# One written list of steps for the work ahead of ab, and four-square scores for pairs 2 to 4

## The chip, the cores and the metric

The kernel runs on one core of a Trainium2 chip, in one launch. The metric is the device time of that launch in microseconds (us); lower is better. The kernel before takes 846.54 us (median of 3 runs, 845.32 to 847.07).

## The reference

Inputs are q, k, v of 4 batches, 8 heads, 576 positions and 64 channels, and six float32 weight matrices, which the host lays out as 64-bit words. Cut to what is computed:

```python
scores = q @ k.T / sqrt(64) - slope[h] * abs(i - j)     # only 0 <= i - j < 128 counts
attn = softmax(scores) @ v                              # 4 x 8 x 576 x 64
x = attn as (2304, 512)
h = (x @ w1) * (x @ w2) @ w3                            # 2304 x 1024
x = h @ w_out                                           # 2304 x 512
h = x @ w_in                                            # 2304 x 2048
out = (h * clip(h + 3, 0, 6) / 6) @ w_out2              # 2304 x 512
```

## The kernel before

Heads are taken two at a time, so there are 16 pairs `n`, four to a batch; 64 channels of one head and 64 of the other fill the 128 partitions. Tokens go through the dense layers in five chunks of 512 (the last of 256), and a chunk needs the four pairs of its batch.

For a pair, `products` (L148 to L163) computes scores in 64-row squares: query square i against the up to three key squares that its window reaches, nine squares i for two heads, in two parts (squares 0 to 5 and 6 to 8), one PSUM tile each (`s`). Each is a 64 by 64 use of the TensorE array, placed by `tile_position`. For pairs 0 to 4 head h sits on rows and columns h of the array, so two corners of the array are used. From pair 5 on, a second copy of q and k with the two heads exchanged (`other`, tiles `qo` and `ko`, filled by two half transfers each) serves the odd squares i, so all four corners are in use. `scores` (L167) adds the position bias and finds the minimum on VectorE (tile `mn`), then ScalarE exponentiates (`pr`). `normalize` (L180) takes a reciprocal on VectorE (`rc`) and multiplies on GpSimd. `pt` (L198) transposes the probabilities by 64 by 64 matmuls against an identity and copies them out of PSUM (`th`, one half by ScalarE, one by VectorE). `pv` (L224) multiplies by v (`X`), copies the sum out (`xf`), and `x_parts` splits it into a high and a low float32r part (`x`). The `s`, `pt` and `X` tiles of all pairs share three PSUM tiles of two banks, by `bank2`.

Dense products are done as three float32r matmuls (`mm3`, L52 to L55: high by high, high by low, low by high). Weights come as 64-bit words: `unpack` (L57 to L74) makes float32 from them with one ScalarE instruction (L66) and two on VectorE (L67, L71); `split` (L76) then makes the two parts, one copy on ScalarE (L77) and one subtraction on VectorE (L78).

Ahead of the first dense chunk w3 and w_out are multiplied into one matrix W: eight row blocks (`w_half`, L383 to L398, tile `wps`, two PSUM banks in turn shared with `ab`), each in two halves; blocks 0 and 1 by plain float32 (L393), 2 to 7 by `mm3`. Then for chunk k the loop `block` gives pieces of `ab_unit` (two products of x by w1 and w2, tile `ab`; the first is copied to `asb` by ScalarE, the second multiplied with it on VectorE and split into `g`) and `y_unit` (g by W, tile `y`), with the next batch's pairs put between the pieces by `gaps`. After three such chunks and two without attention the last layers follow (`h` and `o`).

What sets the order: within `block` TensorE's instructions keep the order in which the code is written. Ahead of `ab`, in the part that this change is about, the order of every engine is left to a scheduler, which ranks the instructions of `attn_slot` and of the list `work` by its own cost model; `work` and `FILL` only say in which order the code hands them over. DMAs are issued by SyncE (SP), one after another; an issue that waits holds those behind it. A raw weight tile (`raw`) is one of three buffers.

Of the kernel before, what the change touches and what calls it, by code (L numbers as in the profile page):

```python
# [23 lines left out]
def tile_attention_moe_moe2(ctx: ExitStack, tc: tile.TileContext, qT, kT, vm, vt, wo, w3, w12, w2x, out):  # L24
# [26 lines left out]

    def mm3(ps, lh, ll, rh, rl, first, last, pinned=False, **kw):  # L52
        in_order(pinned, nc.tensor.matmul(ps, lh, rh, start=first, stop=False, **kw))  # L53
        in_order(pinned, nc.tensor.matmul(ps, lh, rl, start=False, stop=False, **kw))  # L54
        in_order(pinned, nc.tensor.matmul(ps, ll, rh, start=False, stop=last, **kw))  # L55

    def unpack(raw, out=None, pinned=False):  # L57
# [8 lines left out]
        in_order(pinned, nc.scalar.activation(w1f, w1f, AF.Prelu, scale=2.0 ** -112, alpha=-(2.0 ** 32)))  # L66
        in_order(pinned, nc.vector.tensor_scalar(  # L67
# [63 lines left out]
    other = {}  # L131
# [47 lines left out]

    def normalize(n, js):  # L180
        _, sm, rc = stat[n]
        cols = slice(js[0], js[-1] + 1)
        nc.vector.tensor_scalar_add(rc[:, cols], sm[:, cols], 1e-9)
        nc.vector.reciprocal(rc[:, cols], rc[:, cols])
        for i in js:
            o = prob[n, i][:, SPAN - width(i) :]
            nc.gpsimd.tensor_scalar(  # L187
                out=o, in0=o, scalar1=rc[:, i : i + 1], scalar2=1.0, op0=ALU.mult, op1=ALU.mult
            )
# [8 lines left out]
    def pt(n, g):  # L198

        t = bank2(n, 2 - 2 * g, f"pt_{n}_{g}")  # L200
# [5 lines left out]
        for pair in zip_longest(*blocks):  # L206
            for ik in pair:
                for h in range(2):
# [8 lines left out]
                    ))  # L217
        ths = [a1.tile([P, 2 * SPAN], F32, tag="th", bufs=4, name=f"th_{n}_{h}_{g}") for h in range(2)]
        for h in range(2):
            (nc.vector.tensor_copy if h else nc.scalar.copy)(ths[h], t[:, h, 0 : 2 * SPAN])  # L220
        pts[n, g] = ths

    def pv(n):
# [23 lines left out]
        x = a1.tile([P, S], F32, tag="xf", bufs=NP + 1, name=f"xf_{n}")  # L247
        nc.scalar.copy(x, X[0][:, 0:S])
        nc.vector.tensor_tensor(out=x[:, D:S], in0=X[1][:, D:S], in1=x[:, D:S], op=ALU.add)
        x_parts(n, x)  # L250
# [22 lines left out]
    SLOTS = 6  # L273

    def loads(n, nm):
        if n != NP - 1 and n + 1 < NHP:
            load_hp(n + 1 if n >= NP else n + 2, nm)

    def attn_slot(g):
        n, s = divmod(g, SLOTS)  # L280
        if s == 0:
            if n > 0:
                pv(n - 1)
            products(n, 0)
            scores(n, (0, 1, 2))
        elif s == 1:
            normalize(n, (0, 1, 2))
            if 0 < n < NP:
                load_hp(n + 1, "v")
            scores(n, (3, 4, 5))  # L290
            products(n, 1)
        elif s == 2:
            normalize(n, (3, 4, 5))
            scores(n, (6, 7, 8))
            normalize(n, (6, 7, 8))
        elif s in (3, 4):
            pt(n, s - 3)
            loads(n, "qk"[s - 3])

    def pair_steps(n):  # L300

        if n == NP:
            yield from (lambda s=s: attn_slot(SLOTS * n + s) for s in (2, 3, 4))
        else:

            def first():
                for part in range(2):
                    products(n, part)
                for js in ((0, 1, 2), (3, 4, 5), (6, 7, 8)):
                    scores(n, js)  # L310
                    normalize(n, js)

            def second():
                pt(n, 0)
                loads(n, "q")
                pt(n, 1)
                loads(n, "k")

            yield first
            yield second  # L320
        yield lambda: pv(n)
# [12 lines left out]
    def load_wo(i):  # L334
        rawt["wo", i] = rawo[i // 2][:, i % 2, :]
        nc.sync.dma_start(out=rawt["wo", i], in_=wo[i])

    def load(key, src, *pools):
# [4 lines left out]
        nc.sync.dma_start(out=rawt[key], in_=src)  # L343
# [40 lines left out]
    def w_half(i, half):  # L384
# [6 lines left out]
        for m in range(half * KH, (half + 1) * KH):  # L391
            if i < WHOLE:
                nc.tensor.matmul(ps[:, 0:DM], w3v[i][:, m, :], wof[m], start=m == 0, stop=m == KF - 1)  # L393
                continue
            hi, lo = w3v[i]
            mm3(ps[:, 0:DM], hi[:, m, :], lo[:, m, :], *wov[m], m == 0, m == KF - 1)
        if half == 1:
            split(W["h"][:, i, :], W["l"][:, i, :], ps[:, 0:DM], nc.vector)  # L398

    load_hp(0, "qk")  # L400
# [13 lines left out]
    queue = [("w3", i) for i in range(KF)] + [("w12", f) for f in range(W12_EARLY)]  # L414
    nxt = 0

    def more():
        nonlocal nxt
        if nxt < len(queue):
            k, i = queue[nxt]  # L420
            load((k, i), {"w3": w3, "w12": w12}[k][i], rawp, rawp, rawx)
            nxt += 1

    more()
    load_hp(1, "qk")
    load_wo(0)
    load_hp(0, "v")
    load_wo(1)
    load_hp(1, "v")
    more()  # L430
    load_wo(2)
    load_wo(3)
    more()

    work = []
    for i in range(KF):
        work += [("w3", i), ("h", i, 0), ("h", i, 1)]
    head = work.index(("w3", 2))
    work[:head] = [
        ("w3", 0), ("wo", 0), ("wo", 1), ("h", 0, 0), ("w3", 1), ("h", 1, 0),  # L440
        ("wo", 2), ("wo", 3), ("h", 0, 1), ("h", 1, 1),
    ]
    a = work.index(("h", WHOLE - 1, 1)) + 1
    work[a:a] = [("ws", i) for i in range(KH)]
    for f in range(W12_EARLY):
        work.insert(work.index(("h", KH + 1 + f, 1)) + 1 if f < KH - 1 else len(work), ("w12", f))
# [492 lines left out]
```

## Time and profile before

| | us |
|---|---|
| median of 3 runs | 846.54 |
| the profiled execution | 845.8 |
| its span, first to last instruction | 844.0 |
| TensorE busy in the span | 824.2 (98%) |
| VectorE busy | 466.4 (55%) |
| ScalarE busy | 378.4 (45%) |
| GpSimd busy | 98.1 (12%) |
| start of the first `ab` matmul | 100.47 |

The profile counts a matmul as busy from its issue to its modelled end, and matmuls are pipelined, so that consecutive ones overlap. Busy time alone thus doesn't tell how fast TensorE works; the starts of the rows and the granted clock (1.00 is 2.4 GHz, 0.50 is 1.2 GHz) do. A float32 matmul is recorded twice or more, so a pair's 18 score matmuls are 36 records.

### The profile page before, as it was taken

The numbers are of one execution on the slowest core, as the hardware profiler recorded it, in microseconds if no ns is written. First come the engines' busy times: TensorE is split into PE (matmuls) and PEld (weight loads), VectorE is DVE, ScalarE is ACT, GpSimd is POOL, SyncE is SP. The second block draws the span as 40 slices with busy tenths as digits, with TensorE's granted clock in tenths as the row PEclk, the third lists the DMA queues.
The fourth block names the chain that finished last, engine by engine and source line by source line (L and its number), as shares of the span: only waits on it lengthen the run. The fifth ranks groups of instructions, "written<-read, shape, count | busy, mean of one in ns | idle before, by whom it ended". The sixth has DMA issues, their size and how long they took to land.

```text
span 844.0 us, 15817 instructions
## 1 busy us (share of the span) xinstructions
PE 824.2 (98%) x6304; PEld 698.5 (83%) x6304; DVE 466.4 (55%) x1054; ACT 378.4 (45%) x820; POOL 98.1 (12%) x185
## 2 busy tenths in 40 slices
PE   5989999999999999999999999999999999999998
PEld 4567777888888788888899898998889889898886
DVE  5985477425452454246573877885543547443543
ACT  7765565525441445224352654555332335332333
POOL 3333303222231222300000000000000000000000
PEclk9989999999999999999999999999999999999999
DMA  9753543334332332316666589589855377455502
GB/s 352 284 217 100 162 137 102 99 100 114 95 91 73 104 81 62 125 64 237 261 194 239 229 333 363 160 303 390 326 196 215 138 274 293 189 208 203 188 1 75
DMA packets 42841, 155.62 MB, mean 184 GB/s; under 512 B 4880, under 2 KB 20240, under 8 KB 31504
## 3 DMA queue, kind: packets, MB, share of 16 engines
q1 hardware_dynamic: 42768, 154.62, 51.2%
q8 instruction: 49, 0.80, 0.4%
q14 instruction: 24, 0.20, 0.1%
HBM read 118.55 MB, written 36.04 MB: 183 GB/s over the span
## 4 chain that ended last, share of the span: by engine, by line
PE 91%; DVE 4%; ACT 2%; DMA 1%; issue 1%; POOL 0%; SPq 0%; DVEq 0%; POOLq 0%
PE ab L53 8%; PE o L54 8%; PE o L55 8%; PE o L53 8%; PE ab L54 8%; PE ab L55 7%; PE h L53 7%; PE h L54 7%; PE h L55 7%; PE y L53 4%; PE y L54 4%; PE y L55 4%; PE s L159 3%; PE X L241 3%; PE pt L214 3%; DMA raww<-in_w_dram 1%
## 5 line engine op out<-in xcount | busy, mean ns | idle before, releaser
L53 PE MATMUL ab<-x,w12h 128*128 128x512 f32 (+1 forms) x320 | 121.3, 379 | 0.4 <-ACT asb L517 0.4
L54 PE MATMUL ab<-x,w12h 128*128 128x512 f32 (+1 forms) x320 | 118.1, 369 | 0.0
L55 PE MATMUL ab<-x,w12l 128*128 128x512 f32 (+1 forms) x320 | 117.9, 369 | 0.0
L53 PE MATMUL h<-yh,va 128*128 128x384 f32 x336 | 114.1, 340 | 0.2 <-DVE rl L748 0.2
L54 PE MATMUL h<-yl,va 128*128 128x384 f32 x336 | 113.3, 337 | 0.3 <-DVE yl L78 0.3
L55 PE MATMUL h<-yh,va 128*128 128x384 f32 x336 | 113.3, 337 | 0.0
L54 PE MATMUL o<-vo,g 128*128 128x512 f32 x288 | 113.2, 393 | 0.0
L53 PE MATMUL o<-vo,g 128*128 128x512 f32 x288 | 113.1, 393 | 0.0
L55 PE MATMUL o<-vo,g 128*128 128x512 f32 x288 | 87.2, 393 | 0.0
L187 POOL TENSOR_SCALAR pr<-pr,rc 128x192 f32<-128x192 f32 (+1 forms) x144 | 71.9, 519 | 131.5 <-ACT pr L178 79.1
L747 ACT ACTIVATE rl<-c,three 128x384 f32<-128x384 f32 x72 | 44.4, 617 | 79.5 <-DVE c L777 48.4
L53 PEld LDWEIGHTS ab<-x,w12h 128*128 128x128 f32 x320 | 60.4, 189 | 14.3 <-issue 2.0
L178 ACT ACTIVATE pr<-pr,mn 128x192 f32<-128x192 f32 (+1 forms) x144 | 61.3, 427 | 19.8 <-DVE mn L173 19.7
L55 PEld LDWEIGHTS ab<-x,w12l 128*128 128x128 f32 x320 | 60.4, 189 | 10.2
L53 PEld LDWEIGHTS h<-yh,va 128*128 128x128 f32 x336 | 63.1, 188 | 6.7 <-DVE rl L748 3.1
L54 PEld LDWEIGHTS ab<-x,w12h 128*128 128x128 f32 x320 | 60.4, 189 | 9.0
L54 PEld LDWEIGHTS h<-yl,va 128*128 128x128 f32 x336 | 63.1, 188 | 4.2 <-DVE yl L78 0.6
L55 PEld LDWEIGHTS h<-yh,va 128*128 128x128 f32 x336 | 63.1, 188 | 0.0
L55 PEld LDWEIGHTS o<-vo,g 128*128 128x128 f32 x288 | 53.9, 188 | 10.5 <-DVE g L78 0.3
L78 DVE TENSOR_TENSOR g<-rl,g 128x384 fp32r<-128x384 f32 x96 | 53.2, 555 | 16.8 <-ACT g L77 14.3
L53 PEld LDWEIGHTS o<-vo,g 128*128 128x128 f32 x288 | 54.1, 188 | 9.5 <-ACT g L77 0.2
L54 PEld LDWEIGHTS o<-vo,g 128*128 128x128 f32 x288 | 54.1, 188 | 9.3
(95 smaller groups left out, 1371.4 us busy)
## 6 DMA issues: line engine op xcount, KB each, us to landing
va<-vad SPq DMA_DIRECT2D x18, 1792.0 KB, 7.4
vo<-vod SPq DMA_DIRECT2D x18, 1024.0 KB, 9.5
raww<-in_w_dram SPq DMA_DIRECT2D x16, 1024.0 KB, 4.9
rawv<-in_w2x_dram SPq DMA_DIRECT2D x16, 1024.0 KB, 7.4
vad<-va SPq DMA_DIRECT2D x8, 1792.0 KB, 7.3
vod<-vo SPq DMA_DIRECT2D x8, 1024.0 KB, 10.9
yraw<-yT SPq DMA_DIRECT2D x21, 384.0 KB, 9.1
qw<-in_qT_dram SPq DMA_DIRECT2D x16, 288.0 KB, 3.9
```

What stands on the lines that cost most here:

```text
L53: in_order(pinned, nc.tensor.matmul(ps, lh, rh, start=first, stop=False, **kw))
L54: in_order(pinned, nc.tensor.matmul(ps, lh, rl, start=False, stop=False, **kw))
L55: in_order(pinned, nc.tensor.matmul(ps, ll, rh, start=False, stop=last, **kw))
L78: lo_eng.tensor_tensor(out=lo, in0=src, in1=f32(hi), op=ALU.subtract)
L159: in_order(written[0] or (a, h, i % 2) != (0, 0, 0), nc.tensor.matmul(o[HB[h], :], q[HB[r], i * D : (i + 1) * D], k[HB[r], (i + 1) * D - w ...
L178: nc.scalar.activation(o, o, AF.Exp, bias=mn[:, i : i + 1], scale=-1.0, accum_out=sm[:, i : i + 1])
L187: nc.gpsimd.tensor_scalar(out=o, in0=o, scalar1=rc[:, i : i + 1], scalar2=1.0, op0=ALU.mult, op1=ALU.mult)
L214: last_pe["pt", n, g] = in_order(written[0], nc.tensor.matmul(t[HB[c], h, o : o + D], prob[n, i][HB[h], (k - i + 2) * D : (k - i + 3) * D] ...
L241: last_pe["x", n, h] = in_order(written[0] or begun, nc.tensor.matmul(X[p][HB[h], a * D : b * D], vw[place(n)][HB[p], k // 2, HB[h]], pts[ ...
L747: nc.scalar.activation(rl, h, AF.Relu, bias=three[:, 0:1], scale=1.0)
```

## The change

1. `fx` pins instructions to the order in which they are written, on all engines. What `attn_slot`, `work`, `FILL` and `GATE` handed to the scheduler becomes one string of steps, `STEPS`, that is run from left to right; each engine keeps the order of the list. The letters: Lq, Lk, Lv, Lo, L, Lw load q, k, v, w_out, w3 and w12; S is `products`, M `scores`, R `normalize`, P the transposes and T their copies, X the product with v, E its copy, D its split; Uo, U, Uw unpack and Vo, V, Vw split weights; H is half a block of W and Z its split. S2.1 is part 1 of pair 2, M and R have three squares each, H4.0 is the first half of block 4.
2. `unit` functions are cut in two so that unpacking and splitting, transposes and copies, product and copy are steps of their own.
3. q and k are stored in DRAM in both head orders side by side; from pair 2 on one transfer brings both (576 KB instead of 288 KB). `qw` and `kw` have twice the size, `other` is gone.
4. `swap` holds from pair 2 on (before: from pair 5 on).
5. In `block`, pair 4 comes with its scores done, and `gaps` change for pairs 4 to 7.

The diff, cut to this:

```diff
+    fixed = [False]
+    def fx(ins):
+        return in_order(fixed[0], ins)
...
-        qw.append(pool.tile([P, S], F32, name=f"qw{i}"))
-        kw.append(pool.tile([P, S], F32, name=f"kw{i}"))
+        qw.append(pool.tile([P, 2, S], F32, name=f"qw{i}"))
+        kw.append(pool.tile([P, 2, S], F32, name=f"kw{i}"))
...
-                nc.sync.dma_start(out=r[place(n)], in_=src[n])
-                if n > NP:
-                    for h in range(2):
-                        nc.sync.dma_start(out=other[nm][HB[h], :], in_=src[n][HB[1 - h], :])
+                orders = slice(0, 2 if n > 1 else 1)
+                fx(nc.sync.dma_start(out=r[place(n)][:, orders, :], in_=src[n][:, orders, :]))
...
-                    swap = n > NP and i % 2 == 1
+                    swap = n > 1 and i % 2 == 1
                     r = 1 - h if swap else h
-                    q, k = (other["q"], other["k"]) if swap else (qw[place(n)], kw[place(n)])
+                    q, k = (t[place(n)][:, int(swap), :] for t in (qw, kw))
...
+    STEPS = """
+        Lk0 Lq0 S0.0 S0.1 M0.0 Lk1 Lq1 M0.1 R0.0 M0.2 S1.0 R0.1 R0.2 L0 U0 Lo0 Uo0 Lo1 P0.0 P0.1 T0.0
+        Uo1 T0.1 L1 Lv0 U1 H0.0 M1.0 X0 M1.1 R1.0 Lo2 Lo3 L2 R1.1 Uo2 E0 Uo3 H1.0 S1.1 M1.2 Lk2 Lq2 P1.0
+        T1.0 H0.1 S2.0 R1.2 Lv2 Lv1 L3 P1.1 H1.1 Lk3 U2 Vo1 Z0 V2 T1.1 X1 U3 Vo0 Vo2 Lq3 Z1 Vo3 L4 H2.0
+        H2.1 E1 V3 D0 M2.1 L5 M2.0 R2.1 S2.1 Lv3 M2.2 H3.0 R2.0 S3.0 H3.1 P2.0 R2.2 P2.1 U4 U5 V4 Z2 Z3
+        H4.0 V5 M3.0 H5.0 L6 L7 T2.1 H4.1 M3.1 R3.1 U6 U7 T2.0 Z4 V6 H5.1 Lq4 R3.0 X2 Z5 Lw0 V7 H6.0 E2
+        S3.1 Lv4 Uw0 Lw1 D1 Lk4 M3.2 H7.0 P3.0 H6.1 R3.2 P3.1 Vw0 D2 Lw2 T3.0 S4.0 Uw1 T3.1 X3 H7.1 Vw1
+        E3 Z6 S4.1 D3 M4.0 M4.2 M4.1 R4.2 Uw2 R4.0 Z7 R4.1 Vw2
+    """
...
+    written[0] = fixed[0] = True
+    for s in STEPS.split():
+        name = s.rstrip("0123456789.")
+        does[name](*map(int, s[len(name) :].split(".")))
+    fixed[0] = False
...
-            steps = list(pair_steps(n))
-            gaps = (3, 1, 1, 1) if n == NP else (4, 1, 1) if n == NP + 1 else (3, 1, 1)
-            for step, gap in zip(steps, gaps):
-                step()
+            late = k == 0
+            if n > NP:
+                first(n, 0)
+                first(n, 1)
+            gaps = (3, 1, 1) if n == NP else (4, 2, 1) if n == NP + 1 else (3, 1 + late, 1)
+            for step, gap in zip((None, second, pv), gaps):
+                if step:
+                    step(n)
                 for _ in range(gap):
                     yield next(work)
```

How instructions move, at the two places that the prediction rests on. First ScalarE around the start of `ab`, in the built program before (`w12h` and `raww_3` are a weight block of `ab`, `Wh` the high part of W, `pr_6` to `pr_8` the last squares of pair 4, `asb` the copy of the first `ab` product):

```order
L77 CAST w12h_1087<-raww_2_933 128x1024
L77 CAST Wh<-wps_964 128x512
L248 COPY xf_1015<-X_2_991 128x576
L77 CAST x_3_1018<-xf_1015 128x512
L77 CAST x_0_1339<-xf_345 128x64
L77 CAST Wh<-wps_1060 128x512
L178 ACTIVATE pr_6_1138,sm_1035<-pr_6_1138,mn_1034 128x192
L178 ACTIVATE pr_7_1141,sm_1035<-pr_7_1141,mn_1034 128x192
L178 ACTIVATE pr_8_1144,sm_1035<-pr_8_1144,mn_1034 128x192
L517 COPY asb_0_1165<-ab_0_0_1152 128x512
```

and the same place in the changed program, from the last six of the nine exponentials of pair 4 on:

```order
L180 ACTIVATE pr_6_1092,sm_1081<-pr_6_1092,mn_1080 128x192
L180 ACTIVATE pr_7_1095,sm_1081<-pr_7_1095,mn_1080 128x192
L180 ACTIVATE pr_8_1098,sm_1081<-pr_8_1098,mn_1080 128x192
L180 ACTIVATE pr_3_1101,sm_1081<-pr_3_1101,mn_1080 128x192
L180 ACTIVATE pr_4_1104,sm_1081<-pr_4_1104,mn_1080 128x192
L180 ACTIVATE pr_5_1107,sm_1081<-pr_5_1107,mn_1080 128x192
L71 ACTIVATE raww_2_999<-raww_2_999 128x1024
L82 CAST Wh<-wps_912 128x512
L484 COPY asb_0_1160<-ab_0_0_1147 128x512
```

The high part of the last W block and the copy `asb` now stand behind all nine exponentials of pair 4 and the unpacking of the third w12 block; before, six of the exponentials and that unpacking were ahead of both.

Second, VectorE where the first weights are unpacked, before (`raww_1` and `raww_2` are w3 blocks, `rawol` the w_out blocks 2 and 3, `wov` unpacked w_out and `wovl` its low part, `th` a copy of transposes of pair 0):

```order
L67 TENSOR_SCALAR raww_1_134<-raww_1_134 128x1024
L183 TENSOR_SCALAR rc_366<-sm_365 128x3
L184 RECIPROCAL rc_366<-rc_366 128x3
L71 SCALAR_TENSOR_TENSOR w3v_226<-raww_1_134 128x1024
L184 RECIPROCAL rc_366<-rc_366 128x3
L78 TENSOR_TENSOR wovl_377<-wov_196,wovh_376 128x1024
L220 COPY th_1_0_263<-pt_0_237 128x384
L67 TENSOR_SCALAR rawol<-rawol 128x1024
L71 SCALAR_TENSOR_TENSOR wov_267<-rawol 128x1024
```

and in the changed program from the last reciprocal of pair 0 on (`raww_0` is w3 block 0, `rawoh` the w_out blocks 0 and 1):

```order
L186 RECIPROCAL rc_146<-rc_146 128x3
L72 TENSOR_SCALAR raww_0_204<-raww_0_204 128x1024
L76 SCALAR_TENSOR_TENSOR w3v_206<-raww_0_204 128x1024
L72 TENSOR_SCALAR rawoh<-rawoh 128x1024
L76 SCALAR_TENSOR_TENSOR wov_211<-rawoh 128x1024
L227 COPY th_1_0_267<-pt_0_216 128x384
L72 TENSOR_SCALAR rawoh<-rawoh 128x1024
L76 SCALAR_TENSOR_TENSOR wov_270<-rawoh 128x1024
L227 COPY th_1_1_275<-pt_1_241 128x384
L72 TENSOR_SCALAR raww_1_278<-raww_1_278 128x1024
L76 SCALAR_TENSOR_TENSOR w3v_282<-raww_1_278 128x1024
```

The copies of pair 0's transposes now stand between the first four unpackings, and no low part is made among them; before, two low parts of w_out and the third to sixth unpacking came ahead of the second copy.

## Rows read from the trace of the kernel before

**Rows 1.** Two stretches: start, length, busy us (records) by engine, granted clock, DMA

```profile
0.00:100.47 100.47, 87.04 (x917) 63.45 (x917) 70.85 (x176) 65.30 (x146) 34.30 (x56) 0.95 0.59 220
100.47:844.00 743.53, 737.20 (x5390) 635.06 (x5388) 395.52 (x879) 313.07 (x674) 63.81 (x129) 1.00 0.51 180
```

**Rows 2.** TensorE's waits over the span: us, times, longest

```profile
PE s L159 <- DMA kw<-in_kT_dram: 4.6, 1, 4.6
PE s L159 <- DVE rc L184: 2.6, 1, 2.6
PE X L241 <- DVE th L220: 2.5, 3, 1.2
PE pt L214 <- POOL pr L187: 2.3, 3, 1.5
PE wps L393 <- DVE wov L71: 2.0, 1, 2.0
```

**Rows 3.** Stretches, counting score instructions alone; first number after length is TensorE

```profile
86.00:88.00 2.00, 1.88 (x24) 1.53 (x24) 0.00 (x0) 0.00 (x0) 1.00 0.00 0
99.30:100.50 1.20, 1.16 (x12) 0.79 (x12) 0.00 (x0) 0.00 (x0) 1.00 1.01 430
145.10:146.70 1.60, 1.59 (x36) 1.28 (x36) 0.00 (x0) 0.00 (x0) 1.00 0.00 1
```

**Rows 4.** Timeline of TensorE: start, length, work, records

```profile
22.97 3.70 PE L393 MATMUL wps<-wov,w3v 128*128 128x512 f32 x8
...
81.20 1.54 PE L241 MATMUL X<-th,vw 64*64 64x192 f32 x40
...
108.86 0.93 PE L214 MATMUL pt<-ident,pr 64*64 64x64 f32 x48
```

**Rows 5.** Stretches around TensorE's idle times, columns as in rows 1

```profile
12.59:17.00 4.41, 4.41 (x46) 3.68 (x47) 3.37 (x10) 3.54 (x9) 4.25 (x7) 0.61 1.01 385
...
18.79:20.79 2.00, 0.00 (x0) 0.00 (x1) 2.00 (x8) 2.00 (x9) 0.00 (x0) 1.00 1.03 418
20.79:23.00 2.21, 2.21 (x11) 0.91 (x11) 2.21 (x7) 1.55 (x2) 1.27 (x2) 1.00 1.01 419
50.03:54.44 4.41, 1.35 (x29) 0.73 (x29) 3.96 (x8) 3.44 (x6) 2.75 (x3) 1.00 0.48 197
54.44:61.30 6.86, 6.86 (x32) 5.26 (x33) 5.27 (x18) 4.32 (x12) 1.47 (x2) 0.50 0.45 153
```

**Rows 6.** The same view from the first `ab` matmul on

```profile
100.47:108.80 8.33, 8.33 (x38) 6.68 (x36) 3.26 (x12) 3.71 (x9) 1.23 (x3) 1.00 0.64 173
```

**Rows 7.** Groups on VectorE and ScalarE ahead of 100.47: busy us, mean ns, idle before

```profile
L173 DVE CUSTOM_DVE_ANT_0 pr<-s,rel 128x192 f32<-128x192 f32 (+2 forms) x42 | 11.5, 327 | 2.3 <-PE s L159 2.1 <-POOL pr L187 0.2
L71 DVE SCALAR_TENSOR_TENSOR raww<-raww 128x1024 int32<-128x1024 int32 x9 | 11.0, 1220 | 0.8 <-ACT raww L66 0.6
L67 DVE TENSOR_SCALAR raww<-raww 128x1024 int32<-128x1024 int32 x11 | 8.7, 794 | 10.2 <-DMA raww<-in_w_dram 10.2
L78 DVE TENSOR_TENSOR w3l<-raww,w3h 128x1024 fp32r<-128x1024 f32 x6 | 7.4, 1234 | 0.6 <-ACT w3h L77 0.6
...
L178 ACT ACTIVATE pr<-pr,mn 128x192 f32<-128x192 f32 (+2 forms) x42 | 17.9, 430 | 6.9 <-DVE mn L173 6.9
L66 ACT ACTIVATE raww<-raww 128x1024 f32<-128x1024 f32 x11 | 13.0, 1178 | 7.6 <-DMA raww<-in_w_dram 7.6
...
L77 ACT CAST Wh<-wps 128x512 fp32r<-128x512 f32 x8 | 4.6, 574 | 2.9 <-PE wps L55 2.9
```

**Rows 8.** Timeline of GpSimd, columns as in rows 4

```profile
12.75 5.22 POOL L187 TENSOR_SCALAR pr<-pr,rc 128x64 f32<-128x64 f32 x9 [10.44 <-DVE rc L184]
21.73 7.52 POOL L187 TENSOR_SCALAR pr<-pr,rc 128x64 f32<-128x64 f32 x6 [3.76 <-DVE rc L184]
```

**Rows 9.** TensorE's waits from 100 us on

```profile
PE X L241 <- DVE th L220: 1.3, 2, 1.1
```

**Rows 10.** Stretch from 32 to 100 us, columns as in rows 1

```profile
32.00:100.00 68.00, 63.74 (x718) 49.24 (x719) 47.87 (x117) 40.64 (x93) 19.88 (x31) 0.95 0.43 149
```

More of the change, by code (lines that the diff above doesn't have):

```diff
@@ L196, in parity, with squares @@
         return 1 if k == NQ - 1 else k % 2
-    def pt(n, g):
-        t = bank2(n, 2 - 2 * g, f"pt_{n}_{g}")
+    ptb = {}
+    def squares(n, g):
+        ptb[n, g] = t = bank2(n, 2 - 2 * g, f"pt_{n}_{g}")
         blocks = ([], [])
@@ L246, in pv, with joined @@
                     begun.add(key)
[L247 to L250, printed above, removed]
+        Xb[n] = X
+    def joined(n):
+        X = Xb.pop(n)
+        xf[n] = x = a1.tile([P, S], F32, tag="xf", bufs=NP + 1, name=f"xf_{n}")
+        fx(nc.scalar.copy(x, X[0][:, 0:S]))
+        fx(nc.vector.tensor_tensor(out=x[:, D:S], in0=X[1][:, D:S], in1=x[:, D:S], op=ALU.add))
+    def pv(n):
+        weighted(n)
+        joined(n)
+        x_parts(n, xf.pop(n))
         if NP <= n < NHP - 1:
@@ L271, in x_parts, with first, second @@
             xs[B, c] = (t[:, c % 2, 0, :], t[:, c % 2, 1, :])
-    SLOTS = 6
     def loads(n, nm):
         if n != NP - 1 and n + 1 < NHP:
[L277 to L321, printed above, removed]
+            load_hp(n + 1, nm)
+    def first(n, part):
+        products(n, part)
+        for js in ((6, 7, 8),) if part else ((0, 1, 2), (3, 4, 5)):
+            scores(n, js)
+            normalize(n, js)
+    def second(n):
+        pt(n, 0)
+        loads(n, "q")
+        pt(n, 1)
+        loads(n, "k")
     flat = lambda t: t.rearrange("p a b -> p (a b)")
@@ L413, in tile_attention_moe_moe2 @@
     nc.gpsimd.memset(three, 3.0)
[L414 to L446, printed above, removed]
@@ L466, in tile_attention_moe_moe2 @@
-    wi = 0
-    end = work.index(("h", KF - 2, 0))
-    for s in range(nslot):
-        attn_slot(s)
-        upto = FILL[s] if s in FILL else FILL[4] + (s + 1 - len(FILL)) * (end - FILL[4]) // (SLOTS * NP - 2 - len(FILL))
-        if s >= SLOTS * NP - 2:
-            upto = work.index(("h", KF - 2, 1)) + 1
-        if s >= SLOTS * NP:
-            upto = len(work)
-        while wi < min(upto, len(work)):
-            do_work(work[wi])
-            wi += 1
+    STEPS = """
[6 more added lines that the diff above has]
+        E3 Z6 S4.1 D3 M4.0 M4.2 M4.1 R4.2 Uw2 R4.0 Z7 R4.1 Vw2
@@ new lines, in tile_attention_moe_moe2 @@
+    """
+    PARTS3 = ((0, 1, 2), (3, 4, 5), (6, 7, 8))
+    does = {
+        "Lq": lambda n: load_hp(n, "q"),
+        "Lk": lambda n: load_hp(n, "k"),
+        "Lv": lambda n: load_hp(n, "v"),
+        "Lo": load_wo,
+        "L": lambda i: load(("w3", i), w3[i], rawp, rawp, rawx),
+        "Lw": lambda f: load(("w12", f), w12[f], rawp, rawp, rawx),
+        "S": products,
+        "M": lambda n, u: scores(n, PARTS3[u]),
+        "R": lambda n, u: normalize(n, PARTS3[u]),
+        "P": squares,
+        "T": copies,
+        "X": weighted,
+        "E": joined,
+        "D": lambda n: x_parts(n, xf.pop(n)),
+        "Uo": wo_unit,
+        "Vo": wo_split,
+        "U": w3_unpack,
+        "V": w3_split,
+        "Uw": w12_unpack,
+        "Vw": w12_split,
+        "H": w_half,
+        "Z": w_row,
+    }
```

95 lines of the change are left out of this document (45 added, 50 removed).

## The prediction

> **What bounds the kernel now.** I read the span in two stretches first. From 100.47 us, where `ab` begins, TensorE is busy all but some 6 us of 744 at granted clock 1.00 [rows 1], and its waits over the whole span that are worth naming lie ahead of that point but for one [rows 2, 9]. So the work after 100.47 is a block of fixed length, and the question is when `ab` begins and what its first pieces wait for. Ahead of it I summed what TensorE has to do at full clock. A pair's scores by two corners take 1.88 for part 0 and 1.16 for part 1, 3.0 together [rows 3]; five pairs make 15.2. Transposes are 0.93 a half, eight halves 7.4; X is 1.54 a pair, four make 6.2; blocks 0 and 1 of W are four halves of 3.70, 14.8 [rows 4]. Blocks 2 to 7 are 144 matmuls; 36 matmuls of that size took 8.33 us, 0.231 each [rows 6], so 33.3. The sum is 76.9, and the first scores can't start before 4.6, when q and k have landed [rows 2]: `ab` could begin at 81.5 and begins at 100.5. The missing 19 us are some 9 of waits (2.6, 2.0, 2.3, 1.2 of X ahead of `ab`, small ones) and the rest slow clock: from 54.44 to 61.30 the clock was 0.50, which costs half of 6.86, 3.4 us, and from 12.59 to 17.00 it was 0.61, 1.7 us more [rows 5]; the first scores run slow too.
>
> **The change, part by part.**
>
> *Four corners for pairs 2 to 4.* All 36 records of a pair take 1.59 where four corners are used [rows 3], against 3.0. Three pairs save 4.4 us of TensorE; as the list later leaves TensorE the bound, I count all of it, inside the sum below.
>
> *Both head orders in one transfer.* Six loads ahead of `ab` grow by 288 KB, 1.8 MB in all. At the 430 GB/s of a full stretch [rows 3] that is 4 us of transfer. They are issued from some 27 us on, and from 32 to 100 us the DMA engines are busy 0.43 of the time [rows 10]. I take nothing; at worst each pair's scores wait for the second 288 KB twice, 1.4 us a pair, 4 in all. From pair 5 on the bytes are the same and issues fewer: nothing.
>
> *The list, to the first half of W.* Pair 0 starts as before at 4.6. VectorE now reduces its scores with no unpacking between; nine exponentials at 0.43 [rows 7], from some 8.7, end near 13. Unpacking starts at 13.2, instead of 8.3. Here the change loses: H0.0 starts at about 17.5, not 15.8, but pair 1's scores start at 11.4, not 12.6.
>
> *The stretch that VectorE bounds, 13 to 46 us.* Up to Vo3, after which block 2 of W can run through, the list gives VectorE eight unpackings of 0.79 + 1.22 [rows 7], 16.1; five low parts of 1.23, 6.2; nine reductions of 0.33, 3.0; eight copies and sums of half the size of a low part, 0.62 by that estimate, 5.0. That is 30.3. To it I add 2.5 for waits on ScalarE, where an unpacking stands behind six exponentials. Vo3 ends near 46. TensorE waits in this stretch (for E0 ahead of S1.1, for pair 1's normalizing ahead of P1.0, about 1.2 and 2.4), but all that it has to do by then fits. Behind VectorE's waits stand only its own steps; SP holds v of pair 1 and block 3 of w3 behind Lv2, which waits for X0 at 23, and they are needed at 40 and 38. Bounds for this stretch come from GpSimd: pair 0's nine multiplications took 0.58 each, while six of pair 1's took 1.25 each beside unpacking that kept VectorE fully busy [rows 8]. The list puts pairs 0 and 1 beside unpacking throughout. I take 0.58 for pair 0, which is multiplied mostly before the unpacking starts, and 1.25 for the six of pair 1 that stand beside it; all 18 at 0.58 would give Vo3 at 44, all 18 at 1.25 near 51, since the copies T wait for the transposes, these for GpSimd, and the unpacking behind T on VectorE for both.
>
> The Trainium skill has a rule that speaks against this placement: in "SBUF — State Buffer", section "SBUF: two separate sides", VectorE and GpSimd share one port pair, an exclusive lock, so that whoever comes second is blocked for the whole instruction. The 1.25 of rows 8 agrees with it; carried through for both pairs it is the slower rival below.
>
> *From there to `ab`: TensorE.* After 46.0 it has the second half of H2.1, 2.8; ten halves of 12 matmuls, 27.7; S2.1, S3 and S4 by four corners, 3.7; four transposes, 3.7; two X, 3.1. Sum 41.0. VectorE's remaining steps up to E3 are about 30 us beside it, so TensorE should bound; I add 1 us for V4 and Z2, which H4.0 waits for, and for X3. `ab` begins at 88.0, 12.5 earlier than before.
>
> *A wait that the change adds.* The second product of `ab` takes the PSUM bank that the copy `asb` empties. In ScalarE's row that copy now stands behind all nine exponentials of pair 4, an unpacking, and the high part of W's last block, and ScalarE is in order. The exponentials follow D3, at 87.7: nine at 0.44 end at 91.7; the unpacking takes 1.18, the high part 0.57 [rows 7], the copy about the same: 94.1. The first product (12 matmuls, 2.8) ends at 90.8. TensorE stands for 3.3 us; what is queued behind it is all of `ab`. Bounds are 2.7 (three exponentials done ahead of S4.1) and 4.6 (ScalarE late by another step). The second product starts at 94.1; before, it started at 100.5 + 2.7 = 103.2 without a wait. 9.1 are left.
>
> *The clock.* Rows 5 show both answers to an idle TensorE: 2.0 us of idle (18.79 to 20.79) left the clock at 1.00, while 3.1 us idle out of 4.41 (50.03 to 54.44) was followed by 6.86 us at 0.50. The changed program has two places of the second kind, around P1.0 (3.6 idle out of 4.6) and the wait above (3.3). I count one drop, 3.4 us: 9.1 - 3.4 = 5.7.
>
> In "TensorE: Matmul & The Clock Gate", section "Part 1: The HAM clock gate", the skill says that half rate is the default and that activity releases it. By that rule both places would drop, and the time would be the one of the two-drop rival below.
>
> *`gaps`.* X of pair 5 waited 1.3 us for its copies [rows 9], with one piece between transposes and X; now there are two, so 1.0 comes back. Pair 4's X comes two pieces earlier, its copies then have one piece, 2.8 us, against two copies and an unpacking: 0 to 0.5 lost. I count 1.0 in all: 5.7 + 1.0 = 6.7.
>
> The profiled execution was 845.8, its span 844.0 and 1.8 around it; the median is 846.54. 845.8 - 6.7 is 839.1, the median less 6.7 is 839.8. I forecast **839.5 us**.
>
> **Rivals.**
> 1. *No drop of the clock.* The waits are short of what lowered it at 50 to 54 us, or fall apart: 3.4 less, 836.1; with the short bounds of the wait and of GpSimd (0.6 and 2) 833. For it: the 2.0 us idle without a drop. Against: 3.3 is nearer to 3.1 out of 4.41.
> 2. *Two drops*: the stretch to 46 ends 2.6 later (H0.1 at half clock holds Z0 and what is behind it), and `ab` is slow too: 842 to 843.
> 3. *GpSimd held off through pairs 0 and 1*: slower. Each T on VectorE then waits for transposes that wait for 1.25 us multiplications; Vo3 comes at 51 instead of 46, `ab` at 93; with the two drops (6.0 against 3.4) the sum is 6.7 - 5 - 2.6 = -0.9, and with the long bound of the `asb` wait, -2.2: 847 to 848. It decides if block 2's second half starts later than about 52. For it: rows 8, second row. Against: pair 0 has a start of 3 us on the unpacking.
> 4. *Four squares don't run at once* in the new places: 4.4 lost, 844. Against it: pairs from 5 on are written alike and take 1.59 [rows 3].
>
> **How the numbers follow.** Forecast 0.45 (837 to 841.5), no drop 0.27, two drops 0.14, GpSimd 0.09, four squares 0.05. The range reaches down to rival 1 with its short bounds, 832.5, and up past rivals 2 and 4, 845.0; it leaves out rival 3 and the ends. 0.2%, 1.7 us, is about what a measurement of this kernel can tell from no change. Faster by more (under 844.8): the forecast, rivals 1 and 2, half of 4, less a margin, 0.85; within: 0.06; slower: rival 3, 0.09.
>
> **What would show it.** `ab` should begin between 86 and 90; S2 to S4 as 36 records in about 1.6; TensorE waits of 1 to 2.5 us for GpSimd ahead of pair 1's transposes, and of 2.7 to 4.6 for the copy `asb` at the second product of `ab`; a stretch of 6 to 7 us at 0.50 behind one of them; X of pair 5 without a wait; from pair 8 on nothing changed. I am wrong if Vo3 ends after 50, if the DMA is what TensorE waits for, or if the part from `ab` on changes in length by more than these waits and the clock.

## The result, and the profile after

The changed kernel takes 838.46 us (median of 4 runs, 837.42 to 839.42), the kernel before 845.93 beside it (4 runs, 844.83 to 847.07): a ratio of 0.991, 95% interval 0.989 to 0.993. That is 7.5 us faster. The forecast was 839.5, in a range of 832.5 to 845.0. The number was right; the experiments below show that several of its terms were not, and that they partly cancelled.

The profiled execution took 837.42 with a span of 835.5. Read as [rows 1], in two stretches around the first `ab` matmul:

```profile
0.00:88.92 88.92, 79.03 (x916) 56.67 (x917) 68.53 (x162) 60.32 (x136) 36.46 (x50) 0.96 0.67 248
88.92:835.50 746.58, 738.60 (x5390) 635.58 (x5388) 400.99 (x892) 316.91 (x685) 67.21 (x135) 1.00 0.49 181
```

`ab` begins 11.6 us earlier, and what follows is 3.1 us longer: the gain was made ahead of `ab`, and a part was handed back behind it. TensorE's waits over the span, against [rows 2] (us in total, times, longest):

```profile
PE s L161 <- DMA qw<-in_qT_dram: 4.5, 1, 4.5
PE pt L218 <- POOL pr L189: 3.2, 4, 1.5
PE ab L58 <- ACT asb L484: 2.4, 2, 2.3
PE X L255 <- DVE th L227: 1.7, 2, 1.0
```

The waits for `rc` and `wov` are gone, one of 2.3 for the copy `asb` is new, and pair 0's transposes now wait for GpSimd, 2.5 in all (before, only later pairs' did). Where the clock was low, read as [rows 5]:

```profile
12.50:15.98 3.48, 1.76 (x81) 1.49 (x81) 3.24 (x6) 3.48 (x4) 3.48 (x5) 1.00 0.99 415
15.98:22.65 6.67, 5.91 (x34) 3.02 (x35) 6.46 (x16) 2.38 (x8) 1.24 (x1) 0.50 1.03 417
22.65:26.00 3.35, 3.35 (x49) 1.89 (x49) 2.23 (x10) 3.35 (x11) 1.86 (x5) 0.98 1.00 409
91.93:94.19 2.26, 0.00 (x1) 0.00 (x0) 0.96 (x1) 2.21 (x5) 1.02 (x3) 1.00 0.68 277
94.19:97.94 3.75, 3.75 (x9) 2.93 (x10) 2.71 (x7) 1.15 (x1) 3.03 (x6) 0.54 0.00 0
```

Two stretches at 0.50: one of 6.8 us (its end lies in the third row) behind the idle time in pair 0's transposes, one of 3.4 us behind the wait for `asb`. ScalarE's row at that wait (timeline: start, length, work):

```profile
91.65 0.44 ACT L180 ACTIVATE pr<-pr,mn 128x192 f32<-128x192 f32 x1
...
92.09 1.11 ACT L71 ACTIVATE raww<-raww 128x1024 f32<-128x1024 f32 x1
93.09 0.57 ACT L82 CAST Wh<-wps 128x512 fp32r<-128x512 f32 x1
93.56 0.58 ACT L484 COPY asb<-ab 128x512 f32<-128x512 f32 x1
```

and TensorE's there and at the first half of W:

```profile
15.85 0.65 PE L218 MATMUL pt<-ident,pr 64*64 64x64 f32 x16 [1.54 <-POOL pr L189]
17.27 0.69 PE L218 MATMUL pt<-ident,pr 64*64 64x64 f32 x12 [0.76 <-POOL pr L189]
17.89 6.12 PE L388 MATMUL wps<-wov,w3v 128*128 128x512 f32 x8
...
34.51 1.10 PE L161 MATMUL s<-kw,qw 64*64 64x64 f32 x24
...
48.27 0.87 PE L161 MATMUL s<-kw,qw 64*64 64x192 f32 x12
...
94.19 0.57 PE L58 MATMUL ab<-x,w12h 128*128 128x512 f32 x1 [2.26 <-ACT asb L484]
...
107.50 1.54 PE L255 MATMUL X<-th,vw 64*64 64x192 f32 x40 [0.99 <-DVE th L227]
```

The copy stands behind the last exponential, an unpacking and `Wh`, as the order said. At half clock the first half of W takes 6.12 for what took 3.70 [rows 4].

### The profile page after: what moved, and what is told of

Read it like the earlier page. It is cut to its first block, busy times and chain, and to the rows that moved or that the text cites. A ratio compares the mean times of both kernels' runs of the same rounds, so it can differ in the third digit from the quotient of the medians.

```text
span 835.5 us, 15720 instructions
## 1 busy us (share of the span) xinstructions
PE 817.6 (98%) x6304; PEld 692.2 (83%) x6304; DVE 469.5 (56%) x1054; ACT 377.2 (45%) x820; POOL 103.7 (12%) x185
## 4 chain that ended last, share of the span: by engine, by line
PE 87%; DVE 7%; ACT 4%; issue 1%; POOL 1%; DMA 0%; SPq 0%; DVEq 0%; ACTq 0%; POOLq 0%
PE o L59 8%; PE o L60 8%; PE o L58 8%; PE ab L58 8%; PE h L58 7%; PE ab L59 7%; PE ab L60 7%; PE h L59 7%; PE h L60 7%; PE y L58 4%; PE y L59 4%; PE y L60 4%; PE s L161 3%; PE X L255 2%; ACT pr L180 2%; PE pt L218 2%
## 5 line engine op out<-in xcount | busy, mean ns | idle before, releaser
L189 POOL TENSOR_SCALAR pr<-pr,rc 128x192 f32<-128x192 f32 (+1 forms) x144 | 76.1, 549 | 116.2 <-ACT pr L180 91.2
```

The costliest lines, as they stand in the source:

```text
L189: fx(nc.gpsimd.tensor_scalar(out=o, in0=o, scalar1=rc[:, i : i + 1], scalar2=1.0, op0=ALU.mult, op1=ALU.mult))
```

## Experiments

All times below are medians; the kernel before took 845.4 to 846.4 beside them. Where ratios matter they are to the kernel before. The theory on record was that of the prediction: shorter scores, an order that lets TensorE bound from 46 us on, and two prices for it (the wait for `asb`, the clock).

### Is it the four corners?

```diff
-                    swap = n > 1 and i % 2 == 1
+                    swap = n > NP and i % 2 == 1
```

> The changed kernel with scores of pairs 2 to 4 on two corners again, all else the same, the transfers of both head orders too. Theory (TensorE bounds from 46 us on): S2, S3 and S4 take 3.0 us each instead of 1.6 to 2.0, `ab` begins 3.6 to 4.4 later, and the time is 842 to 843. Rival (VectorE or ScalarE sets the end of that stretch, four corners only make TensorE wait): 838.5 to 840. TensorE's waits for other engines ahead of `ab` don't change by the theory; by the rival they shrink by what the scores grow.

The second adds, in `load_hp`:

```diff
-                orders = slice(0, 2 if n > 1 else 1)
+                orders = slice(0, 2 if n > NP else 1)
```

> As e1_two_corners, and the loads of q and k for pairs 2 to 4 bring one head order, 288 KB instead of 576. Theory (the doubled transfers are hidden): within 0.5 us of e1_two_corners. Rival (the second 288 KB holds other loads on SP's queue): 1 to 4 us faster than e1_two_corners.

The third makes the same part of the change in the kernel before, and nothing else (`qw` and `kw` of twice the size, both orders by one transfer from pair 2 on, `swap` from pair 2 on):

> The kernel before with one part of the change alone: q and k in both head orders by one transfer, and four corners for the scores of pairs 2 to 4. Its order ahead of `ab` is still the scheduler's. Theory (after e1_two_corners: what the scores save ahead of `ab` mostly goes into waits, and the order makes the gain): 844 to 846, `ab` begins 0 to 1.5 earlier than in the kernel before. Rival (the step of the prediction: 3 times 1.4 of TensorE time come off the end): 841 to 842, `ab` begins 4 earlier.

Measured: 838.92 (837.43 to 840.72), 837.84 (837.37 to 837.97), and 847.17, which is slower than the kernel before (ratio 1.0031, interval 1.0014 to 1.0047). The changed kernel's 838.46 lies between the first two. TensorE's rows of e1_two_corners at the scores of pairs 2 and 3:

```profile
48.50 1.20 PE L161 MATMUL s<-kw,qw 64*64 64x192 f32 x12
52.58 1.90 PE L161 MATMUL s<-kw,qw 64*64 64x64 f32 x24
...
90.29 0.50 PE L58 MATMUL ab<-x,w12h 128*128 128x512 f32 x1
```

A pair's scores take 1.90 + 1.20 on two corners and 1.10 + 0.87 on four, 1.1 apart and not 1.4. From S2.1 to `ab` it is 41.8 us in e1 and 40.65 in the changed kernel (48.27 to 88.92), so of the 2.6 that the scores of that stretch grew (two parts by 0.8, three by 0.33) 1.15 arrived at `ab`; the wait of X of pair 3 (0.68) took part of the rest. The 0.8 by which S2.0 grew went into the wait for GpSimd behind it: from S2.0 to the second half of block 1 of W it is 2.97 in e1 and 2.98 in the changed kernel. With one head order (e2) the same stretch is 41.80, 47.67 to 89.47: the doubled transfers cost nothing. In the whole time the four corners can't be told from 0, by either e1 or e2: the intervals of e1 and of the changed kernel leave room for some 3.5 us at most. The runs of e1 lie in two pairs (837.4 and 837.8, 840.1 and 840.7), and the trace is of the slowest, so what it shows behind `ab` is no measure of the corners. Without the list they bring nothing: in e5 `ab` begins at 100.7. The rival of e1 holds for the time, and e5 came out even slower than its theory: this is not where the gain is.

### Is it the pinned order?

```diff
-    written[0] = fixed[0] = True
+    written[0] = fixed[0] = False
     for s in STEPS.split():
```

> The changed kernel with the same list of steps, written in the same order, but not pinned: a scheduler ranks the instructions ahead of `ab`, as in the kernel before. Theory (the pinned order of the list makes most of the gain): 842 to 846; unpacking comes back in front of pair 0's multiplications and of its copies, and TensorE's waits ahead of `ab` grow by 4 or more. Rival (the finer steps and their place in the code are enough, the pin adds nothing): 837.5 to 839.5.

Measured: 844.58 (ratio 0.9992, interval 0.9983 to 1.0001): without the pin the same steps in the same order of writing, four corners included, give nothing. The theory holds, and the pin is worth 6 to 7 us (6.1 by the medians; each was taken beside runs of its own of the kernel before, and by the ratios it is 6.8). The next two pin half of the list each; `S2.0` is the point of change:

```diff
         does[name](*map(int, s[len(name) :].split(".")))
+        if s == "S2.0":
+            written[0] = fixed[0] = False
```

> The changed kernel, pinned to the list only up to and with S2.0, the first scores of pair 2; the steps behind it are written in the same order, and a scheduler ranks them. Theory (after e6_unpinned, where S2.0 came at 44.5 instead of 34.5 and `ab` at 100.9 instead of 88.9: the gain is made ahead of S2.0, where unpacking stands behind pair 0's and pair 1's steps on VectorE): S2.0 at 34 to 36, `ab` at 89 to 92, 837 to 840. Rival (the order behind S2.0 makes it): `ab` at 98 or later, 842 to 845.

> The mirror of e9_pin_first: ranked by a scheduler up to S2.0, pinned behind it. Theory: S2.0 at 42 to 45, `ab` at 97 to 100, and then the wait for `asb` as in the changed kernel: 843 to 847. Rival: `ab` at 91 or earlier, 838 to 840.

Measured: 848.16 (ratio 1.0024, interval 1.0011 to 1.0036) and 843.45 (0.9965, 0.9954 to 0.9976). Starts in the profiled runs, and the length from `ab` to the end of the span:

| | S1.1 | S2.0 | `ab` | from `ab` on |
|---|---|---|---|---|
| before | 42.2 | 48.9 | 100.5 | 743.5 |
| unpinned | 35.8 | 44.5 | 100.9 | 741.6 |
| pinned up to S2.0 | 38.9 | 46.9 | 104.1 | 741.6 |
| pinned behind S2.0 | 31.5 | 36.0 | 95.2 | 746.5 |
| the whole list | 29.1 | 34.5 | 88.9 | 746.6 |

Only the column `ab` compares like with like, for all of W stands ahead of it in every row. Ahead of S2.0 stand three halves of blocks 0 and 1 in the last two rows and all four in the others, 3.7 us more, and in the kernel before also 41 matmuls of later blocks, 9.5 us at the 0.231 of [rows 6]. My theory of e9 fell: with its own steps pinned, S2.0 came 12.4 us later than with the whole list, 3.7 of it for that half block, and with only the later steps pinned 1.5 later. VectorE's rows tell why. The two copies of pair 0's transposes and the sum of its X in the changed kernel (timeline):

```profile
16.84 0.55 DVE L227 COPY th<-pt 128x384 f32<-128x384 f32 x1
...
19.24 0.55 DVE L227 COPY th<-pt 128x384 f32<-128x384 f32 x1
...
26.90 0.68 DVE L267 TENSOR_TENSOR xf<-X,xf 128x512 f32<-128x512 f32 x1
```

and in e9_pin_first, with what stands ahead of the copies (the last row is ScalarE's):

```profile
17.92 1.23 DVE L83 TENSOR_TENSOR wovl<-wov,wovh 128x1024 fp32r<-128x1024 f32 x1 [1.11 <-ACT wovh L82]
19.06 0.55 DVE L227 COPY th<-pt 128x384 f32<-128x384 f32 x1
...
22.65 1.23 DVE L83 TENSOR_TENSOR wovl<-wov,wovh 128x1024 fp32r<-128x1024 f32 x1 [1.11 <-ACT wovh L82]
23.79 0.55 DVE L227 COPY th<-pt 128x384 f32<-128x384 f32 x1
...
34.16 0.68 DVE L267 TENSOR_TENSOR xf<-X,xf 128x512 f32<-128x512 f32 x1
...
26.99 1.17 ACT L71 ACTIVATE raww<-raww 128x1024 f32<-128x1024 f32 x1 [2.94 <-DMA raww<-in_w_dram]
```

A pin keeps pinned instructions in order among themselves; an unpinned one may still stand between them. The low parts `wovl`, which no TensorE instruction needs before block 2 of W, come ahead of each copy of pair 0 and cost it 1.2 of work and 1.1 of waiting for ScalarE, twice. With that VectorE reaches pair 1's scores 4.6 later (26.19 for 21.63). ScalarE then takes the unpacking of the third w3 block, U2, ahead of pair 1's exponentials, when its transfer lands at 27.0, and pair 1's GpSimd work starts 6.4 us later:

```profile
30.14 4.71 POOL L189 TENSOR_SCALAR pr<-pr,rc 128x64 f32<-128x64 f32 x6 [13.04 <-DVE rc L186]
```

(23.74 in the changed kernel, below). The kernel before and e6_unpinned have low parts in the same place; there the second of these two copies starts at 33.12 and 27.32:

```profile
23.93 0.55 DVE L220 COPY th<-pt 128x384 f32<-128x384 f32 x1
33.12 0.55 DVE L220 COPY th<-pt 128x384 f32<-128x384 f32 x1
```

In e10_pin_last no low part stands there; its time lies in the range that I gave only by luck, for the reason falls with that of e9, and its `ab` is late for what happened behind S2.0: 2.7 of waits for GpSimd in pair 1's transposes instead of 0.76, and a low clock from 39.7 to 46.5, in which half a block of W took 6.20.

What the pin does, by these rows, is keep weight work that is needed late behind attention work that is needed early, on VectorE and ScalarE. No run pins one engine alone, so the share of each, and of the order of the DMA issues, stays open. The table's last column shows the price of the pinned end: some 5 us between the two kinds of order.

### The price behind `ab`

```diff
-        E3 Z6 S4.1 D3 M4.0 M4.2 M4.1 R4.2 Uw2 R4.0 Z7 R4.1 Vw2
+        E3 Z6 S4.1 D3 M4.0 Z7 M4.2 M4.1 R4.2 R4.0 R4.1 Uw2 Vw2
```

> The changed kernel with the split Z7 of W's last block moved up in the list, behind M4.0 instead of behind R4.0, and Uw2 behind R4.1. The second product of `ab` then no longer waits for the copy `asb` behind nine exponentials and an unpacking. Theory (the wait of 2.3 us and the 3.4 us of half clock behind it, worth 1.7, both come from that order): no wait at the second product, no stretch at 0.50 near 95, time 834 to 835. Rival 1 (the clock drop has another cause): 836. Rival 2 (the wait only moves on to the transposes of pair 4, whose exponentials now end 0.6 to 1.2 later, or to the third weight block, which is unpacked later): 837 to 839.

and with only Z7 moved:

```diff
+        E3 Z6 S4.1 D3 M4.0 Z7 M4.2 M4.1 R4.2 Uw2 R4.0 R4.1 Vw2
```

> As e3_z7_early, but Uw2 stays ahead of R4.0, so that the third weight block is unpacked and its buffers come free as early as in the changed kernel; only Z7 is moved. Theory (in e3_z7_early the 2.6 us wait of S5.1 came from the later transfers of the next weight blocks, whose unpacking stands on ScalarE ahead of the copy of X4): no wait of S5.1 over 0.5, 833.5 to 835. Rival (it came from the order that the scheduler then gives ScalarE after the list, whatever the transfers do): a wait of 1.5 to 3 for that copy again, 836 to 837.

Measured: 836.35 (835.61 to 836.51) and 839.12 (838.94 to 840.19). In e3 the wait at the second product is gone, and two others are there (waits, then the stretch behind the first of them):

```profile
PE s L161 <- ACT xf L266: 2.6, 1, 2.6
...
PE ab L58 <- ACT asb L484: 0.9, 1, 0.9
```

```profile
109.08:115.00 5.92, 5.92 (x27) 4.57 (x28) 5.32 (x23) 4.34 (x15) 1.52 (x2) 0.71 0.72 226
```

The medians differ by 2.1, and no run of e3 is as slow as the fastest of the changed kernel. But the two traces are only 1.2 apart (834.3 and 835.5), and 0.85 of that lies ahead of `ab`, which begins at 88.07, where the two lists are alike and the first low stretch lasted 3.4 us instead of 6.8. From `ab` on it is 746.2 for 746.6. So rival 2, that the wait moves on, took nearly all of the 4 us in the traces; the low clock now follows the 2.6. Where the rest of the 2.1 comes from they don't show. ScalarE's row shows what the copy `xf` of pair 4 stands behind:

```profile
103.59 1.16 ACT L71 ACTIVATE raww<-raww 128x1024 f32<-128x1024 f32 x1 [3.91 <-DMA raww<-in_w_dram]
104.91 0.62 ACT L82 CAST g<-asb 128x512 fp32r<-128x512 f32 x1 [0.16 <-DVE asb L490]
106.05 1.12 ACT L82 CAST w12h<-raww 128x1024 fp32r<-128x1024 f32 x1 [0.51 <-DVE raww L76]
107.32 1.21 ACT L71 ACTIVATE raww<-raww 128x1024 f32<-128x1024 f32 x1
108.42 0.61 ACT L266 COPY xf<-X 128x576 f32<-128x576 f32 x1
```

In e8 that wait is 1.0, ScalarE waits for the next weight block until 105.6, later still than the 103.6 of e3, and three other waits came (1.0 for GpSimd at pair 4's transposes, 0.7 and 1.3 for `asb`). Neither theory nor rival of e8 holds; what sets the landing of those blocks is open.

### `gaps`

```diff
-            gaps = (3, 1, 1) if n == NP else (4, 2, 1) if n == NP + 1 else (3, 1 + late, 1)
+            gaps = (3, 1, 1) if n == NP else (4, 1, 1) if n == NP + 1 else (3, 1, 1)
```

> The changed kernel with the `gaps` of before for pairs 5 to 7, (4, 1, 1) and (3, 1, 1): one piece instead of two between the transposes and X. Theory (the step of the prediction): X of pair 5 waits 1.0 to 1.3 for its copies again, 839.5. Rival (the wait of X only moves, to the scores behind it): 838 to 838.8.

Measured: 838.69 (837.80 to 841.33), the changed kernel's time. X of pair 5 waits 0.17, not 1.0 to 1.3, and its row takes 2.00 instead of 1.55, some 0.6 in all; the wait of 1.0 ahead of X of pair 4 stays:

```profile
129.57 2.00 PE L255 MATMUL X<-th,vw 64*64 64x192 f32 x44 [0.17 <-DVE th L227]
```

The theory falls: with the list in place the second piece buys nothing that the time shows.

### The idle time in pair 0, GpSimd and the clock

`F` stands for matmuls of the identity by itself into a tile that nobody reads.

```diff
-        Lk0 Lq0 ... Uo0 Lo1 P0.0 P0.1 T0.0
+        Lk0 Lq0 ... Uo0 Lo1 P0.0 F8 P0.1 T0.0
```

> The changed kernel with eight matmuls of 128 by 128 float32 (the identity by itself, into a PSUM bank that is free then, read by nobody) between the two halves of pair 0's transposes, in the 1.5 us that TensorE idles there. Theory (that idle time is what lowered the clock from 16.0 to 22.7): granted clock 1.00 from 11 to 26 us, the first half of W's block 0 takes 3.7 us instead of 6.1, and since TensorE runs without a break from there on, `ab` begins 1.5 to 2.4 earlier: 836 to 837. Rival 1 (the clock is right but VectorE sets the pace up to 46 us): clock 1.00, `ab` at the same time within 0.7, 838 to 838.5. Rival 2 (the clock falls for another reason): still 0.50 from 16 on, 838.5 or more.

```diff
-            fx(nc.gpsimd.tensor_scalar(
+            fx((nc.vector if n == 0 else nc.gpsimd).tensor_scalar(
```

> The changed kernel with pair 0's nine multiplications on VectorE instead of GpSimd, all else in the same order. Theory (GpSimd, held off by VectorE's unpacking, is what TensorE waits for in pair 0's transposes): the waits of 0.2, 1.5 and 0.8 us for GpSimd are gone, but VectorE has 1 to 2 us more ahead of the first unpacking, so the first half of W starts at 17.5 to 19 and the time is 838 to 840. Rival (GpSimd's multiplications bound the start of W): the first half of W starts at 15 to 16.5, 836 to 837.

e4: 839.0, with 836.06 to 841.58 the widest spread of all. The profiled run is the fastest one; its clock:

```profile
8.81:10.82 2.01, 0.00 (x0) 0.03 (x1) 1.87 (x14) 2.01 (x11) 0.72 (x3) 1.00 1.01 428
11.00:14.40 3.40, 3.40 (x48) 3.18 (x49) 2.46 (x6) 3.21 (x8) 3.00 (x6) 0.50 1.01 426
14.40:26.00 11.60, 11.60 (x159) 7.39 (x153) 10.17 (x27) 7.51 (x19) 4.67 (x7) 1.00 1.02 412
```

With the hole filled the clock was 1.00 from 14.4 on, but low before, behind 2.0 us of idle ahead of S1.0, which the filling can't touch. X of pair 0 began 2.5 earlier, pair 1's second transposes waited 2.1 for GpSimd instead of 0.76, and `ab` began at 87.9, 1.05 earlier. So in this trace 2.4 us of slow clock there are worth 1 at `ab`; between theory and rival 1. In the median nothing is gained. The spread of the other three runs, of which there is no trace, is unexplained: by my estimate their mean granted clock, 0.994 to 0.995 for 0.996 in the fastest, covers up to 1.7 us of the 5.5.

e12: 839.48 (838.44 to 840.95). The waits for GpSimd in pair 0 are gone, and the first half of W starts at the old place, since it now waits for the unpacked w_out:

```profile
17.68 1.98 PE L388 MATMUL wps<-wov,w3v 128*128 128x512 f32 x4 [1.17 <-DVE wov L76]
```

The theory holds: GpSimd fills a time that VectorE's unpacking bounds anyway. What a faster GpSimd alone would give this run doesn't show, since the nine multiplications take VectorE 2.2 us.

### Z7 early, and matmuls ahead of the first scores

The order of e3_z7_early with five matmuls ahead of the first scores:

```diff
-        Lk0 Lq0 S0.0 S0.1 ...
+        Lk0 Lq0 F5 S0.0 S0.1 ...
```

> e3_z7_early with five matmuls of 128 by 128 float32 (the identity by itself, read by nobody) ahead of the first scores, from 2 us on, where TensorE waits for q and k. Theory (the first scores take 4.4 to 5.4 instead of 3.0 because the clock is low at first, though the records say 1.00; work ahead of them brings the clock up sooner, and VectorE and ScalarE, which bound the stretch to 46 us, follow): the first scores take 3.0 to 4.0, `ab` begins 1 to 1.5 earlier than in e3_z7_early, 834.5 to 835.5. Rival (something else slows the first scores, or the weights' transfers bound what follows): 836 to 836.8.

Measured: 835.37 (834.93 to 835.91; ratio 0.9875, interval 0.9859 to 0.9892), 3.1 faster than the changed kernel. Against e3 it is 1.0 by the medians, but the ranges overlap and so do the intervals (0.9859 to 0.9892, 0.9873 to 0.9906): that step isn't shown.

```profile
2.01 2.50 PE L423 MATMUL fill<-ident 128*128 128x128 f32 x10 [2.01 <-POOL ident masks.py:199]
4.63 4.05 PE L161 MATMUL s<-kw,qw 64*64 64x64 f32 x36
10.69 1.65 PE L161 MATMUL s<-kw,qw 64*64 64x64 f32 x21 [2.01 <-issue]
```

The first scores took 4.05 against 4.65 in e3, and `ab` began 0.4 earlier, less than the 1 to 1.5 of the theory; the first scores are still slower than 3.0. Without the five matmuls they took 4.30 to 5.41 in the other traces, so that 4.05 is their doing is likely and not shown.

## Why the prediction was right, and where it was not

**What bounds.** Right: from the scores of pair 6 on, both kernels take the same (698.9 and 699.3 us to the end of the span), and all that changed lies ahead.

**Four corners, 4.4.** The step that failed. Mis-sized first: the 1.59 of [rows 3] is one run of 36 records, while the list has the two parts apart, 1.10 + 0.87; a pair saves 1.1. And counted as if TensorE alone bounded: e1 and e2 show 1.15 of it between S2.1 and `ab`, nothing at S2.0, and in the whole time nothing that can be told from 0. (Of the 4.4 only 3.5 stand in the sum behind 46 us, which has no S2.0.) That sum came out near all the same (`ab` at 88.9 for 88.0): block 2 of W was 0.5 further on by then than I took (Vo3 ended at 44.7, for 46), and what follows took 1.4 longer, 0.7 of it the wait of X of pair 3.

**The gain was put to the wrong part.** The prediction summed what the engines have to do in the pinned order, gave 4.4 of the 12.5 to the corners, and had no term for the pin itself. e6, e9 and e10 show that it carries the result: four corners and finer steps without it give 844.6.

**Transfers, 0.** Right, by e2.

**To the first half of W.** Right: 17.89 for 17.5, pair 1's scores at 11.04 for 11.4, unpacking from 12.77 for 13.2.

**VectorE's stretch.** Its end was right, Vo3 at 44.7 for 46. The prices for GpSimd were not: 0.58 was taken for pair 0, and its nine took 0.72 each (1.07 + 5.42), the last six 0.90; of pair 1's six, for 1.25, each took 1.00. GpSimd's rows, the last from a place where VectorE does nothing beside it:

```profile
10.32 1.07 POOL L189 TENSOR_SCALAR pr<-pr,rc 128x64 f32<-128x64 f32 x3 [8.01 <-ACT pr L180]
11.79 5.42 POOL L189 TENSOR_SCALAR pr<-pr,rc 128x192 f32<-128x192 f32 x6 [0.40 <-DVE rc L186]
23.74 1.07 POOL L189 TENSOR_SCALAR pr<-pr,rc 128x64 f32<-128x64 f32 x3 [6.52 <-ACT pr L180]
25.20 2.48 POOL L189 TENSOR_SCALAR pr<-pr,rc 128x192 f32<-128x192 f32 x3 [0.40 <-DVE rc L186]
33.53 3.53 POOL L189 TENSOR_SCALAR pr<-pr,rc 128x192 f32<-128x192 f32 x3 [5.85 <-ACT raww L71]
...
162.50 3.48 POOL L189 TENSOR_SCALAR pr<-pr,rc 128x64 f32<-128x64 f32 x9 [3.55 <-ACT pr L180]
```

The wait of 1.2 ahead of S1.1 did not come, the 2.4 ahead of P1.0 came as 0.76 at P1.1, and 2.5 that I had not named came in pair 0. By the Trainium skill ("SBUF — State Buffer", section "SBUF: two separate sides") GpSimd is blocked while VectorE holds the shared port pair; nine multiplications in 6.49 and 7.08 beside unpacking against 3.48 from 162.50 agree with it. Rival 3, with 1.25 for all 18, did not come: they took 0.75 on average, and pair 0's cost little (e12).

**The wait for `asb`.** Right in place: 2.26 for 3.3, only because `ab` came 0.9 later than forecast; the second product started at 94.19 for 94.1, 9.1 ahead of the kernel before. The cause has a link that the prediction doesn't name. In the kernel before and in e3 the second product starts before the copy `asb` does (103.32 for 103.52, 90.92 for 91.70), so it takes the other bank, that of the last W block. In the changed kernel that block's low part is made only after the second product has begun, so of the two banks only that of `asb` came free in time:

```profile
94.66 0.66 DVE L83 TENSOR_TENSOR Wl<-wps,Wh 128x512 fp32r<-128x512 f32 x1
```

That undoing it gives 4 us, as I then expected of e3, was wrong: 2.1 came back by the medians, and 0.4 behind `ab` in the traces.

**The clock.** One drop of 3.4 was counted. There were two low stretches, of which the first stood at 16 and not around P1.0, was in no sum, and was worth about 1 (e4). The second lasted 3.4 us and cost 1.6 (nine matmuls 0.43 apart instead of 0.23), half of the term. By the Trainium skill ("TensorE: Matmul & The Clock Gate", section "Part 1: The HAM clock gate") half rate is the default and activity releases it; that both low stretches stand behind idle time (1.7 us in 2.1, and 2.26) agrees with it. Which idle time is followed by a low stretch the rows alone don't say: the 2.0 of [rows 5] was not, and the same wait for `asb`, 2.25 to 2.27, was followed by one here, in e2, e7 and e10 and by none in e1 and e12, where the clock stayed at 1.00 for the next 3.4 us. So that one drop came behind this wait was partly luck.

**`gaps`, 1.0.** Wrong by e7; X of pair 4 lost 1.0 where 0 to 0.5 was allowed, and X of pair 5 would have lost some 0.6 without it.

From the second product of `ab` on the forecast lost 2.4 of its 9.1 (3.4 less 1.0), and 0.6 was lost: 1.6 of clock and 1.0 for X of pair 4, less 1.7 of waits that the kernel before has there (1.3 in [rows 9] and 0.4 for an `asb`) is 0.9; the 0.3 between them I leave unplaced. So the forecast was 1 us too slow, the clock's term being double its size. That it came so near is in part luck, since the clock's term erred one way, and `gaps` and the corners the other.

## What to carry to other kernels

An order written down pays by what it keeps out: look which late work stands ahead of early work on the engine that bounds (here low parts and unpacking of weights ahead of steps of the first pairs), and pin that late work too, for a pin on the early steps alone keeps nothing out. A saving on an engine counts only for the part that isn't waiting already; two kernels with one part of the change each, old order with new scores and new order without pin, would have shown it before any sum. Where a pinned list ends, read each engine's last rows: a long in-order tail (nine exponentials and an unpacking ahead of a copy) is paid by the next stage, and moving one step of it up may only move the wait (e3, e8).

## What the runs showed of the hardware

- Low stretches of the granted clock were 3.4 or 6.8 us long in every trace (3.4 and 6.8 in the kernel before, 6.8 and 3.4 after), one at the very end of the span left out, and the same code had them at other places from run to run: kernels that are alike up to 80 us showed the first from 16.0 to 22.8 (after), for 3.4 us from 18.5 (e3) or from 35.8 (e8). By that I estimate that a run moves by 1 to 2 us (3.4 us more at half clock cost up to 1.7), and differences below that need several runs.
- The first scores take 4.05 to 5.41 us for the same 36 records, while the granted clock reads 1.00; on two corners at full speed it is 3.0 [rows 3]. Whether the record misses a low clock there or something else holds them, no run shows.
- The same multiplication of 128x192 takes VectorE 0.26 us a piece (0.78 for three, e12). GpSimd takes nine, of which seven have that size, in 3.48 us where VectorE does nothing beside it, and in 6.49 and 7.08 beside unpacking.
